# Statistics of four row tiles moved to ScalarE, exponentials in groups of eight, and another order of all pieces

## The chip, the cores and the metric

The kernel runs on one NeuronCore of a Trainium2 chip. Five engines run side by side, each with a queue of its own: TensorE (PE in the profile, with its weight loads as PEld), VectorE (DVE), ScalarE (ACT), GpSimd (POOL) and SyncE (SP, which here only issues DMAs). The metric is the device time of one execution in microseconds.

## The reference, cut to what matters

```python
mod = (_silu(c) @ w_mod).reshape(1, 6, 1, -1)           # sa, ca, ga, sb, cb, gb
h = _layernorm(x) * (1 + ca) + sa                        # x is 2048 x 512
# S4: K[d, l] = Re sum_n C[d,n] exp(dt[d] A[d,n] l) dt[d] B[d,n],   N = 128
# y = irfft(rfft(h, 4096) * rfft(K, 4096))[:2048] + h * Dskip
x = x + ga * y
h = _layernorm(x) * (1 + cb) + sb
r = max(h @ w1 + b1, 0)                                  # w1 512 x 1792
x = x + gb * ((r * r) @ w2 + b2)                         # w2 1792 x 512
```

`_layernorm` takes mean and variance over the 512 columns of a row; dt is exp(log_dt). All data is float32.

## The kernel before, in words

**Stages.** The program is one list of instructions, written piece by piece, and then put in another order by a planner.

1. *Start.* dt is worked out on VectorE from the load `log_dt` (L541 to L551, ending in `dtc`), spread by PE (L554) and copied by ScalarE (L557). From it come, for the first four of eight blocks of channels (HEAD = 4), the parameters (L577 to L624: on ScalarE an arctangent, L604, and sines, L613 and L615; on VectorE a reciprocal, L601; on POOL products and sums), and tables of exponentials (L866, 24 on ScalarE for each group of blocks). Beside it the load `cin` gives silu(c) (L670 to L684) and the modulation (L679 onward), from which come `g1` and `shift` (L704 on ScalarE, L705 on VectorE).
2. *Rows.* x is held as 16 row tiles of 128x512. For each, VectorE takes mean and variance (L661 BN_STATS, L662 BN_AGGR), and four rows at a time POOL adds eps and takes the power -1/2 (L665, L666). Then for each row VectorE subtracts the mean and multiplies by `g1` (L716), ScalarE scales an identity by the row's rstd (L718, "selection", four buffers), PE multiplies (L720, which waits for `shift` once, and 16 of L723) and ScalarE copies the result out of one of three PSUM banks (L726) into `xj`, a part of the buffer `big`.
3. *Kernel and transforms* (61 to some 280 us). K is made in 32 pieces: POOL adds phases (L847, L875) and multiplies amplitudes (L897, L901), ScalarE takes sine and cosine (L885 to L887), VectorE multiplies (L911 to L914), and PE sums over n (L921). PE's transforms go between them: stage one (L772, copied out by ScalarE at L774), stage two (L782), products on VectorE (L932), and back (L940, copied by VectorE at L946).
4. *Second half.* The inverse (L1129), the second layernorm (L1150 onward), and the feed-forward part in two pairs of 4 row groups: first product L1242, with high and low parts of each operand, bias and squares (L1251 to L1254, and L1287), second product L1263 to L1265, and at each end `block_end` (L1272, L1275 add the input rows).

**What sets the order.** `keep_order` takes the groups of instructions and hands them to the engines in a simulated time: of those that are ready, the one that can begin first, with a cost from `weight` and an urgency from the dictionary `urgent`. That is filled by `hurry` (a whole part) and `push` (one piece, by a key such as "amp 5" or "r3"), with numbers in the tables HURRY, PUSH and EAGER. ORDER says which piece of the transforms is written behind which piece of K. Consecutive exponentials are one group there, however many. Within an engine the chip keeps the order that comes out; between engines semaphores hold it. Dependencies stay as they are written.

```python
 661            nc.vector.bn_stats(sts[s % 4], rows[s])
 662            nc.vector.bn_aggr(mv1[:, s, :], sts[s % 4])
...
 665            nc.gpsimd.tensor_scalar(var, var, EPS, None, op0=ALU.add)
 666            nc.gpsimd.tensor_tensor(var, var, rsq, op=ALU.pow)
```

Of the kernel before, what the change touches and what calls it, by code (L numbers as in the profile page):

```python
# [1477 lines left out]
```

## Time and profile before

| | before |
|---|---|
| median of three runs | 625.21 us (624.66 to 626.1) |
| profiled execution, own time | 623.39 us |
| its span | 621.6 us |
| mean granted TensorE clock | 0.987 |
| busy: PE, POOL | 573.8 us (92%), 458.6 us (74%) |
| busy: DVE, ACT | 442.8 us (71%), 413.3 us (66%) |

The own time is what the device counted for the execution that the profiler watched, and the span is from its first instruction to its last; they differ by 1.8 us. A row of the timeline reads: start in us, duration in us, engine, line, operation, output <- input by the program's names, shapes and types, number of instructions in the row, and, in brackets, how long the engine had stood idle and what released it. A row "x24" holds 24 instructions in succession, and its duration is that of all together. In a window's row stand the stretch, its length, the busy time of each engine with its instructions, the granted clock, the DMA share and the bandwidth.

### The profile page before, as it was taken

The numbers are of one execution on the slowest core, as the hardware profiler recorded it, in microseconds if no ns is written. First come the engines' busy times: TensorE is split into PE (matmuls) and PEld (weight loads), VectorE is DVE, ScalarE is ACT, GpSimd is POOL, SyncE is SP. The second block draws the span as 40 slices with busy tenths as digits, with TensorE's granted clock in tenths as the row PEclk, the third lists the DMA queues.
The fourth block names the chain that finished last, engine by engine and source line by source line (L and its number), as shares of the span: only waits on it lengthen the run. The fifth ranks groups of instructions, "written<-read, shape, count | busy, mean of one in ns | idle before, by whom it ended". The sixth has DMA issues, their size and how long they took to land.

```text
span 621.6 us, 21600 instructions
## 1 busy us (share of the span) xinstructions
PE 573.8 (92%) x9390; PEld 490.8 (79%) x9390; DVE 442.8 (71%) x714; ACT 413.3 (66%) x781; POOL 458.6 (74%) x380
## 2 busy tenths in 40 slices
PE   1479998999999999999899999999998999999996
PEld 1346987999999988998677877788886887778875
DVE  6697588899598979855799845458949645456743
ACT  3868999988978777541878656455966545555341
POOL 5649999999998998350754898935798587794351
PEclk9779999999999999999999999999999999999999
DMA  9941003330311063065441432015444253210432
GB/s 317 398 153 38 36 5 72 71 71 4 72 37 38 13 164 90 20 156 174 139 137 34 119 102 69 17 35 159 146 121 134 84 137 102 55 30 34 135 103 84
DMA packets 45838, 60.70 MB, mean 98 GB/s; under 512 B 5168, under 2 KB 26544, under 8 KB 45616
## 3 DMA queue, kind: packets, MB, share of 16 engines
q1 hardware_dynamic: 45312, 59.20, 32.7%
q8 instruction: 73, 1.20, 0.8%
q10 hardware_dynamic: 432, 0.14, 0.1%
q14 instruction: 21, 0.17, 0.1%
HBM read 46.74 MB, written 4.19 MB: 82 GB/s over the span
## 4 chain that ended last, share of the span: by engine, by line
PE 66%; DVE 16%; ACT 10%; POOL 3%; issue 2%; DMA 2%; SPq 0%; DVEq 0%; ACTq 0%
PE ps L940 8%; PE ac L1242 8%; PE ps L782 6%; PE ps L772 6%; PE ps L1242 4%; PE kg L921 3%; PE ac L1264 3%; PE ac L1263 3%; PE ac L1265 3%; PE ps L1263 3%; PE ps L1265 3%; PE ps L1264 3%; PE ps L723 3%; PE kg L1242 2%; ACT tg L885 2%
## 5 line engine op out<-in xcount | busy, mean ns | idle before, releaser
L1211 POOL TENSOR_TENSOR w2r<-xy,w2r 128x512 fp32r<-128x512 f32 x56 | 80.5, 1438 | 64.3 <-ACT w2r L1210 60.8
L782 PE MATMUL ps<-xy,t_sb 128*64 128x64 f32 x1920 | 63.1, 223 | 1.1 <-DVE xy__761 L932 1.0
L782 PEld LDWEIGHTS ps<-xy,t_sb 128*64 128x64 f32 x1920 | 59.9, 138 | 3.1 <-DVE xy__761 L932 1.3
L940 PE MATMUL ps<-e_sb,xy 128*64 128x128 f32 (+2 forms) x768 | 54.6, 261 | 0.3 <-DVE xy L932 0.3
L1210 ACT CAST w2r<-xy 128x512 fp32r<-128x512 f32 x56 | 34.8, 621 | 27.9 <-DMA xy<-w 13.2
L1264 PE MATMUL ac<-w2r,r 128*128 128x512 f32 x112 | 43.7, 390 | 0.1
L1263 PE MATMUL ac<-w2r,r 128*128 128x512 f32 x112 | 43.6, 390 | 0.0
L1265 PE MATMUL ac<-w2r,r 128*128 128x512 f32 x112 | 43.6, 389 | 0.0
L901 POOL TENSOR_TENSOR rtl<-tables 128x1024 f32<-128x1024 f32 x22 | 43.1, 1957 | 0.0
L1242 PE MATMUL ac<-tt,k1t 128*128 128x512 f32 x168 | 41.8, 393 | 0.6
L940 PEld LDWEIGHTS ps<-e_sb,xy 128*64 128x64 f32 x768 | 40.7, 139 | 1.0 <-DVE xy L932 0.5
L940 PE MATMUL ps<-e_sb,xy__761 128*64 128x128 f32 x384 | 38.1, 277 | 1.9 <-ACT xy L774 1.4
L774 ACT COPY xy<-ps 128x512 f32<-128x512 f32 x60 | 34.2, 595 | 6.8 <-PE ps L772 6.8
L1234 POOL TENSOR_TENSOR k1t<-xy,k1t 128x1024 fp32r<-128x1024 f32 x14 | 34.3, 2450 | 6.0 <-ACT k1t L1232 6.0
L1242 PEld LDWEIGHTS ac<-tt,k1t 128*128 128x128 f32 x168 | 31.1, 188 | 9.0 <-DVE xy L1363 2.7
L875 POOL TENSOR_TENSOR rtl<-lo,big 128x1024 int32<-128x1024 int32 x16 | 34.2, 2139 | 4.9 <-DVE big L946 2.8
L1143 POOL TENSOR_TENSOR big<-big,xy 128x512 f32<-128x512 f32 x12 | 16.6, 1403 | 24.5 <-ACT big L1140 24.3
L946 DVE COPY big<-ps 128x256 f32<-128x256 f32 (+1 forms) x66 | 24.4, 408 | 14.5 <-PE ps L940 14.2
L875 POOL TENSOR_TENSOR llph<-lo,big 128x1024 int32<-128x1024 int32 x16 | 34.5, 2158 | 0.0
L1263 PE MATMUL ps<-w2r,r 128*128 128x512 f32 x84 | 33.6, 400 | 0.0
L772 PE MATMUL ps<-d_sb,ksb 128*64 128x128 f32 x512 | 32.9, 275 | 0.4 <-DVE ksb L1005 0.3
L1265 PE MATMUL ps<-w2r,r 128*128 128x512 f32 x84 | 32.8, 391 | 0.0
(300 smaller groups left out, 1751.5 us busy)
## 6 DMA issues: line engine op xcount, KB each, us to landing
xy<-w SPq DMA_DIRECT2D x91, 256.0 KB, 2.8
xy<-xt SPq DMA_DIRECT2D x32, 256.0 KB, 4.1
xy<-xy SPq DMA_DIRECT2D x32, 256.0 KB, 3.5
xy<-w_mod SPq DMA_DIRECT2D x5, 1024.0 KB, 9.3
out_dram<-p SPq DMA_DIRECT2D x16, 256.0 KB, 2.2
t_sb<-c_t SPq DMA_DIRECT2D x1, 2048.0 KB, 11.6
i2c<-c_i SPq DMA_DIRECT2D x4, 512.0 KB, 4.6
big<-prm SPq DMA_DIRECT2D x2, 768.0 KB, 6.0
```

The source lines that it names most:

```text
L772: nc.tensor.matmul(ps[64 * r : 64 * r + 64, 128 * i : 128 * i + 128], src[:, i], d1_sb[:, r], start=True, stop=True)
L782: nc.tensor.matmul(ps[64 * r : 64 * r + 64, 64 * i : 64 * i + 64].rearrange("p (h q t) -> p q h t", h=2, t=2), t2_sb[:, 8 * g + i, r], src ...
L875: nc.gpsimd.tensor_tensor(ph.rearrange("p d r (a b) -> p (d r) a b", a=4), bc(low_phase[:, us].rearrange("p d r b -> p (d r) b"), 2, 4), b ...
L901: nc.gpsimd.tensor_mul(am[:, 0, :, 32:96].rearrange("p d (v x) -> p d v x", v=2), bc(et[:, 256 + 8 * d0 : 384 + 8 * d0].rearrange("p (y a) ...
L940: nc.tensor.matmul(ps[64 * m : 64 * m + 64], pairs(y)[:, g, i // 2, 64 * m : 64 * m + 64, i % 2], e1_sb[:, h].rearrange("p (r j) -> p r j" ...
L1210: nc.scalar.copy(to[:, 0], wst)
L1211: nc.gpsimd.tensor_sub(to[:, 1], wst, to[:, 0].bitcast(F32))
L1234: v.tensor_sub(to[:, 1, 0:4], sum4, f32(to[:, 0, 0:4]))
L1242: nc.tensor.matmul(ps[:, cols], x, y, start=(i == 0 and not onto), stop=(i == 5), skip_group_check=onto)
L1263: pe.append(nc.tensor.matmul(banks[m], r2l[:, ms], hi_, start=(f == 0), stop=False))
L1264: pe.append(nc.tensor.matmul(banks[m], r2h[:, ms], lo_, start=False, stop=False))
L1265: pe.append(nc.tensor.matmul(banks[m], r2h[:, ms], hi_, start=False, stop=(f == NF - 1)))
```

## The change

1. *Statistics.* For rows 12 to 15 (`ON_ACT = (3,)`, the last four) BN_STATS and BN_AGGR are left out. Two passes of ScalarE with a running sum (`accum_out`) take their place: Identity with scale -1/512 sums to the negated mean, and Square with that as bias sums the squared deviations. What the passes write is scrap, into the part of `xj` that the row's copy fills later. The row product then adds the negated mean, and POOL's first instruction multiplies by 1/512 besides adding eps.
2. *Exponentials.* A group of them is at most eight (`EXP_PART = 8`), so the planner can put other instructions between.
3. *Costs.* Changed in the planner: arctangent counts as being in sine's table; costs of small VectorE and POOL instructions and of float32r matmuls; which instructions share the port of VectorE and POOL; a latency on one engine between a write and its use (`LATE`); a first landing time of 800 ns for loads.
4. *Order.* EAGER, HURRY and PUSH hold other numbers, ORDER is written a little differently, and many pieces get keys of their own: "first", "stats", "rstd", "scale", "shift", "row", "second" in the start, "statistics", "prepare", "apart", "w1", "w2", "squares", "end", "ready" in the second half.

```diff
-EAGER = (-9562, 11339, -94586, 321)
+EAGER = (-66075, -100296, -97238, 981)
 ON_DVE = {}
+ON_ACT = (3,)
 PACED = 2
-HURRY = (-1461, -4821, 8205, 112224, 84830, 415716, 138080, -1155)
+EXP_PART = 8
+HURRY = (-5655, 3681, -27793, 1547244, 582933, 1907014, 158015, -98043)
...
-    "00": -56717, "10": -14679, "30": -7223, "40": -6492, "50": -30466, "60": -22657, "A0": 6594, "A1": 1436,
+    "00": -27019, "10": -1752, "20": 1281, "30": -19704, "40": 6869, "50": 735, "A1": -49404, "A2": 83060,
...
-    return {"Exp": 1, "Sin": 2, "Arctan": 3, "Sqrt": 4}.get(str(getattr(ins, "func", "")).split(".")[-1])
+    return {"Exp": 1, "Sin": 2, "Arctan": 2, "Sqrt": 4}.get(str(getattr(ins, "func", "")).split(".")[-1])
...
-        if of and of[-1][0] == eng and (of[-1][1] is None or (kind and of[-1] == key)):
+        if of and of[-1][0] == eng and (of[-1][1] is None or (kind and of[-1] == key and not (kind == "exp" and len(groups[-1]) >= EXP_PART))):
...
-        nc.vector.bn_stats(sts[s % 4], rows[s])
-        nc.vector.bn_aggr(mv1[:, s, :], sts[s % 4])
+        if s // 4 in ON_ACT:
+            none = xj[:, :, 4 * s : 4 * s + 4].rearrange("p d g -> p g d")
+            row = rows[s].rearrange("p (g d) -> p g d", g=4)
+            nc.scalar.activation(none, row, AF.Identity, scale=-1.0 / D, accum_out=mv1[:, s, 0:1])
+            nc.scalar.activation(none, row, AF.Square, bias=mv1[:, s, 0:1], accum_out=mv1[:, s, 1:2])
+        else:
+            nc.vector.bn_stats(sts[s % 4], rows[s])
+            nc.vector.bn_aggr(mv1[:, s, :], sts[s % 4])
...
-            nc.gpsimd.tensor_scalar(var, var, EPS, None, op0=ALU.add)
+            unit = 1.0 / D if s // 4 in ON_ACT else 1.0
+            nc.gpsimd.tensor_scalar(var, var, unit, EPS, op0=ALU.mult, op1=ALU.add)
...
-            nc.vector.scalar_tensor_tensor(row, row, mv1[:, s, 0:1], g1, op0=ALU.subtract, op1=ALU.mult)
+            away = ALU.add if s // 4 in ON_ACT else ALU.subtract
+            nc.vector.scalar_tensor_tensor(row, row, mv1[:, s, 0:1], g1, op0=away, op1=ALU.mult)
```

Line numbers change with it: the first row matmul is L784 for L720, the row copy L790 for L726, the exponentials L933 for L866, the first sine L658 for L613, stage one L839 for L772, the phase L942 for L875, the kernel product L988 for L921.

**What moves.** The counts on PE, POOL and SP are equal; VectorE has 8 instructions less, ScalarE 8 passes and one table load more (10 loads for 9). Three places show the order.

VectorE in the start, at the chain of dt (`kf`, `fr`, `pl`, `ki`, `dtc`), before:

```order
L546 TENSOR_SCALAR pl<-fr 128x4
L548 SCALAR_TENSOR_TENSOR pl<-pl,fr 128x4 x5
L549 TENSOR_SCALAR ki<-kf 128x4
L548 SCALAR_TENSOR_TENSOR pl<-pl,fr 128x4
L551 SCALAR_TENSOR_TENSOR dtc<-pl,ki 128x4
L661 BN_STATS st_75<-xy_94 128x6
L662 BN_AGGR mv_74<-st_75 128x2
```

and now:

```order
L714 BN_STATS st_76<-xy_94 128x6
L593 SCALAR_TENSOR_TENSOR pl<-pl,fr 128x4
L715 BN_AGGR mv_74<-st_76 128x2
L593 SCALAR_TENSOR_TENSOR pl<-pl,fr 128x4
L714 BN_STATS st_77<-xy_94 128x6
L593 SCALAR_TENSOR_TENSOR pl<-pl,fr 128x4
L714 BN_STATS st_78<-xy_94 128x6
L593 SCALAR_TENSOR_TENSOR pl<-pl,fr 128x4
L715 BN_AGGR mv_74<-st_77 128x2
L715 BN_AGGR mv_74<-st_78 128x2
L596 SCALAR_TENSOR_TENSOR dtc<-pl,ki 128x4
```

The statistics of the first four rows stand between the steps of the chain instead of behind it. On ScalarE's DMA queue `cin` is now issued ahead of `ldt`.

ScalarE behind the cast of `shift` (`big_87` holds `xj`, `ps_160` to `ps_162` are the three banks, `tables` the exponentials), before:

```order
L704 CAST shift<-s_317 128x512
L718 ACTIVATE big_86<-ident,mv_74 128x2x64
L726 COPY big_87<-ps_161 128x128x4
L613 ACT_TABLE_LOAD
L613 ACTIVATE big_86<-big_86 128x4x64
L726 COPY big_87<-ps_162 128x128x4
L726 COPY big_87<-ps_160 128x128x4
L718 ACTIVATE big_86<-ident,mv_74 128x2x64 x3
```

and now:

```order
L764 CAST shift<-s_317 128x512
L711 ACTIVATE big_87,mv_74<-xy_97 128x4x128 x2
L712 ACTIVATE big_87,mv_74<-xy_97,mv_74 128x4x128
L711 ACTIVATE big_87,mv_74<-xy_97 128x4x128
L712 ACTIVATE big_87,mv_74<-xy_97,mv_74 128x4x128 x2
L790 COPY big_87<-ps_161 128x128x4
L782 ACTIVATE big_86<-ident,mv_74 128x2x64
L711 ACTIVATE big_87,mv_74<-xy_97 128x4x128
L933 ACTIVATE tables_336<-big_86 128x64 x8
L782 ACTIVATE big_86<-ident,mv_74 128x2x64
L790 COPY big_87<-ps_162 128x128x4
```

The eight passes (L711, L712) and 16 exponentials stand where the sine was, which now follows 30 rows behind the cast, after two table loads; 16 exponentials and the arctangent's chain, which stood ahead of the cast, now stand behind it.

VectorE at the switch between row groups in the feed-forward part (`p` output rows, `ac` banks, `r` squares), before:

```order
L1275 TENSOR_TENSOR p_4619<-p_4619,big_86 128x512 x2
L1287 SCALAR_TENSOR_TENSOR ac_4764<-ac_4764,b1c,p_4619 128x512
L1186 TENSOR_TENSOR tt<-rawh,tt 128x1024
L1253 TENSOR_TENSOR ac_4764<-ac_4764,xy_95 128x512
L1254 TENSOR_TENSOR r_4615<-ac_4764,r_4615 128x512
```

and now:

```order
L1360 TENSOR_TENSOR p_4619<-p_4619,big_86 128x512
L1372 SCALAR_TENSOR_TENSOR ac_4764<-ac_4764,b1c,p_4619 128x512
L1360 TENSOR_TENSOR p_4619<-p_4619,big_86 128x512
L1337 TENSOR_TENSOR ac_4764<-ac_4764,xy_99 128x512
L1372 SCALAR_TENSOR_TENSOR ac_4762<-ac_4762,b1c,p_4619 128x512
L1338 TENSOR_TENSOR r_4615<-ac_4764,r_4615 128x512
```

The product and difference (now L1337, L1338) no longer stand behind L1186 (now L1267), and the bias step L1287 (now L1372) stands between the two additions.

More of the change, by code (lines that the diff above doesn't have):

```diff
@@ L40 @@
 HEAD = 4
-EAGER = (-9562, 11339, -94586, 321)
+EAGER = (-66075, -100296, -97238, 981)
 ON_DVE = {}
+ON_ACT = (3,)
 PACED = 2
-HURRY = (-1461, -4821, 8205, 112224, 84830, 415716, 138080, -1155)
+EXP_PART = 8
+HURRY = (-5655, 3681, -27793, 1547244, 582933, 1907014, 158015, -98043)
 EXPS = [(0, 1), (1, 1), (2, 2), (4, 2), (6, 2)]
 PUSH = {
[41 rows of a table removed]
[75 rows of a table added]
 }
 ORDER = (
-    "rrrrrrrxrrrxrrrrrrpCABBCCBCBCAACB.BBCBAAAAlAC...0aaaa.1.aDaaa..DbbbbEEDD..DEbxbD.b2DDb.EccccccE."
-    ".FEE3ccF..dddd.EdddFF4d.FGG..FeeGeeFG..GexFGHHe5Ge.w.efffGHf.Hf..fH.wwH6fHfgg.g.gHwg..gg7hhhgh"
+    "rrrrrrrxrrrxrrrrrrpCBABCCBCBCAACB.BBCBAAAAlAC.0..aaaa1..aDaaa..DbbbbEDED..DEbxbD.b2DDb.EccccccE."
+    ".FEE3ccF..dddd.EdddF4Fd.FGG..FeeGeeFG..GeFGHHxe5Ge..efffGHf.Hfw..wfH.wH6fHfggw.g.Hgg..ggg7hhhh"
 ).split(".")
@@ L143, in shares_port @@
     of, to = wide(ins.ins), wide(ins.outs)
-    return type(ins).__name__ != "InstBNStats" and all(of) and any(to) | (len(of) > 1)
+    return type(ins).__name__ not in ("InstBNStats", "InstReciprocal") and all(of) and any(to) | (len(of) > 1)
 def function_table(ins):
-    return {"Exp": 1, "Sin": 2, "Arctan": 3, "Sqrt": 4}.get(str(getattr(ins, "func", "")).split(".")[-1])
+    return {"Exp": 1, "Sin": 2, "Arctan": 2, "Sqrt": 4}.get(str(getattr(ins, "func", "")).split(".")[-1])
 def within(ins):
@@ L166, in weight @@
             if ins.ins[0].bass_ap.dtype == FR:
-                t = max(moving / 2.4 + 13, 119)
+                t = max(moving / 2.4 + 15, 121)
                 t += 340 if any(st == 0 for st, _ in ins.ins[0].ap[1:]) else 0
@@ L185, in weight @@
             if n <= 4:
-                t = 120
+                t = 75
             elif type(ins).__name__ == "InstReciprocal":
                 t = 70 + 6.15 * n
+            elif "TensorScalar" in type(ins).__name__ and shares_port(ins) and sum(free_size(a) > 4 for a in operands(ins.ins)) == 1:
+                t = 65 + 0.55 * n + 60 * sum(free_size(a) == 1 for a in operands(ins.ins)[1:])
             elif type(ins).__name__ != "InstBNStats":
@@ L193, in weight @@
             wide = operands(ins.ins)
-            whole = bool(wide) and all(a.ap[-1][0] == 1 and len(a.ap) == 2 for a in wide)
-            t = 140 + (2.13 if whole else 1.91 if str(wide[0].bass_ap.dtype) == str(I32) else 1.75) * n if wide else 70 + 1.2 * n
+            spread = any(st == 0 and k > 1 for a in wide for st, k in a.ap[1:])
+            t = 140 + (2.16 if not spread else 1.92 if str(wide[0].bass_ap.dtype) == str(I32) else 1.75) * n if wide else 70 + 1.2 * n
+            if n <= 4:
+                t = 1020 if len(wide) > 1 else 230
         case _:
@@ L207 @@
 PACKET, FIRST_END = 127.67, 92.2
+LATE = {"PE": 0, "Activation": 90, "DVE": 120, "Pool": 110, "SP": 0}
 def keep_order(tc, traced, slots, in_turn, whole, urgent, behind, follows):
@@ L252, in keep_order @@
     seen, held, left_by = {}, {}, {}
-    before = [set() for _ in groups]
+    before, tight = [set() for _ in groups], set()
     for g, il in enumerate(groups):
@@ L273, in keep_order @@
                             before[g].add(h)
+                            if w and of[h][0] == of[g][0]:
+                                tight.add((h, g))
                             if write and rows | r == rows and cells | c == cells:
@@ L308, in keep_order @@
             ready[of[g][0]].append(g)
-    landed = table = shape = 0
+    landed, table, shape, pool_port = 800, 0, 0, 0
     port = False
@@ L357, in keep_order @@
             port = shares_port(groups[g][0])
-            cost += max(0, free["Pool"] - now) if port else 0
+            cost += max(0, pool_port - now) if port else 0
         elif e == "Pool":
-            cost += max(0, free["DVE"] - now) if port else 0
+            wide = bool(groups[g][0].outs) and hasattr(groups[g][0].outs[0], "bass_ap") and free_size(groups[g][0].outs[0]) > 4
+            cost += max(0, free["DVE"] - now) if port and wide else 0
+            pool_port = now + cost if wide else pool_port
         elif e == "Activation":
@@ L374, in keep_order @@
         for h in after[g]:
-            at[h] = max(at[h], free[e] if of[h][0] == e and not dma else done + (100 if of[h][0] == "PE" else 0))
+            at[h] = max(at[h], free[e] + (LATE[e] if (g, h) in tight else 0) if of[h][0] == e and not dma else done + (100 if of[h][0] == "PE" else 0))
             left[h] -= 1
@@ L654, in tile_adaln_ssm_ffn @@
     spare = [bank("tg", 2)[:, 0:256] for _ in range(2)]
+    fine = mark
     for _ in parameters(0, HEAD, spare):
-        pass
+        push(fine, "first ")
+        fine = len(nc.cur_bb.bb.instructions)
     hurry(mark, HURRY[0])
-    mark = len(nc.cur_bb.bb.instructions)
+    mark = fine = len(nc.cur_bb.bb.instructions)
     for s in range(16):
-        nc.vector.bn_stats(sts[s % 4], rows[s])
-        nc.vector.bn_aggr(mv1[:, s, :], sts[s % 4])
+        if s // 4 in ON_ACT:
[6 more added lines that the diff above has]
+            nc.vector.bn_aggr(mv1[:, s, :], sts[s % 4])
+        push(fine, "stats ")
+        fine = len(nc.cur_bb.bb.instructions)
         if s % 4 == 3:
             var = mv1[:, s - 3 : s + 1, 1]
-            nc.gpsimd.tensor_scalar(var, var, EPS, None, op0=ALU.add)
+            unit = 1.0 / D if s // 4 in ON_ACT else 1.0
+            nc.gpsimd.tensor_scalar(var, var, unit, EPS, op0=ALU.mult, op1=ALU.add)
             nc.gpsimd.tensor_tensor(var, var, rsq, op=ALU.pow)
+            push(fine, "rstd ")
+            fine = len(nc.cur_bb.bb.instructions)
     hurry(mark, HURRY[1])
@@ L703, in tile_adaln_ssm_ffn @@
             g1[:, 128 * q : 128 * q + 128], ident[:, 32 * q : 32 * q + 1].to_broadcast([P, P]), g4, start=True, stop=True)
+    push(mark, "scale ")
+    fine = len(nc.cur_bb.bb.instructions)
     nc.scalar.copy(shift, bc(s4, 1, 4))
     nc.vector.scalar_tensor_tensor(shift, shift.bitcast(F32), second, bc(s4, 1, 4), op0=ALU.mult, op1=ALU.subtract)
+    push(fine, "shift ")
     hurry(mark, HURRY[3])
@@ L715, in row_pieces @@
             mark = len(nc.cur_bb.bb.instructions)
-            nc.vector.scalar_tensor_tensor(row, row, mv1[:, s, 0:1], g1, op0=ALU.subtract, op1=ALU.mult)
+            away = ALU.add if s // 4 in ON_ACT else ALU.subtract
+            nc.vector.scalar_tensor_tensor(row, row, mv1[:, s, 0:1], g1, op0=away, op1=ALU.mult)
+            push(mark, "row ")
+            fine = len(nc.cur_bb.bb.instructions)
             sel = sels[s % 4]
@@ L726, in row_pieces @@
             moved.append(nc.scalar.copy(xj[:, :, 4 * s : 4 * s + 4], ps.rearrange("p (g d) -> p d g", g=4)))
+            push(fine, "r")
             hurry(mark, HURRY[4])
@@ L737, in parameter_pieces @@
         decay(HEAD, NC - HEAD)
+        fine = mark
         for _ in parameters(HEAD, NC - HEAD, (g1[:, 0:256], g1[:, 256:512])):
-            pass
+            push(fine, "second ")
+            fine = len(nc.cur_bb.bb.instructions)
         more.append(1)
@@ L1046, in tile_adaln_ssm_ffn @@
             next(work[t])
-            push(mark, t)
+            if t not in "pr":
+                push(mark, t)
     w2v = w2.rearrange("(t p) d -> p t d", p=P)
@@ L1145, in inverse, with pushed, wrap, g @@
                     paced_load(xts[s + 4], xt[s + 4])
+    def pushed(key):
+        def wrap(f):
+            def g(*a, **k):
+                mark = len(nc.cur_bb.bb.instructions)
+                r = f(*a, **k)
+                push(mark, key)
+                return r
+            return g
+        return wrap
+    @pushed("statistics ")
     def statistics(s):
@@ L1152, in statistics @@
         nc.vector.reciprocal(rstd2[:, s : s + 1], rstd2[:, s : s + 1])
+    @pushed("prepare ")
     def prepare(s, banks, plain_):
@@ L1182, in tile_adaln_ssm_ffn @@
     b11, b12, b21, b22 = rawh[:, 0, 0:2], rawh[:, 1, 0:2], rawh[:, 0, 2:4], rawh[:, 1, 2:4]
+    @pushed("apart ")
     def apart(to, of):
@@ L1202, in tile_adaln_ssm_ffn @@
     w2_made = {}
+    @pushed("w2 ")
     def w2_tile(n):
@@ L1218, in tile_adaln_ssm_ffn @@
     w1s = {}
+    @pushed("w1 ")
     def w1_sums(g):
@@ L1247, in tile_adaln_ssm_ffn @@
     r2 = {}
+    @pushed("squares ")
     def squares(n, ps, rr, b=None):
@@ L1268, in ffn2 @@
             w2_tile(n + 3)
+    @pushed("end ")
     def block_end(k, banks, xos):
@@ L1384, in tile_adaln_ssm_ffn @@
         block_end(2 * pair, acc_b, [p1[:, i] for i in range(4)])
+        @pushed("ready ")
         def ready(n):
```

114 rows, old and new, of the table PUSH are left out of this document.

## The prediction

> **What bounds the kernel now.** I read the shares first, then the windows by stage, then the timeline where TensorE stands still.
>
> ```profile
> span 621.6 us, 21600 instructions
> PE 573.8 (92%) x9390; PEld 490.8 (79%) x9390; DVE 442.8 (71%) x714; ACT 413.3 (66%) x781; POOL 458.6 (74%) x380
> ...
> core 0: us, PE busy (x) PEld busy (x) DVE busy (x) ACT busy (x) POOL busy (x), PEclk, DMA share, GB/s
> 16.00:31.00 15.00, 6.18 (x84) 4.61 (x76) 10.62 (x22) 13.43 (x53) 9.89 (x14) 0.77 1.06 400
> 47.00:62.00 15.00, 14.29 (x325) 10.27 (x323) 10.75 (x19) 12.17 (x29) 14.12 (x14) 1.00 0.13 35
> 280.00:326.00 46.00, 41.02 (x1355) 33.97 (x1352) 36.02 (x88) 26.42 (x72) 21.49 (x17) 1.00 0.51 150
> ...
> 193.98 2.14 POOL L875 TENSOR_TENSOR rtl<-lo,big 128x1024 int32<-128x1024 int32 x1 [1.74 <-ACT tg L887]
> ```
>
> TensorE is busy for 573.8 of 621.6 us, and the change leaves its matmuls as they are, so only the 47.8 us in which it stands still can be won. Over half of that lies ahead of 47 us, where ScalarE (13.43 of 15 us in the second row) carries the work. In the row stage (third row) PE, ACT and POOL are all nearly full, and POOL stays so until about 250 us: the 1.74 us ahead of the phase at 193.98 is its one real gap. About 5 us more are lost between 280 and 326 us (46.00 less 41.02), and 2.88 us at one place near 477 us, shown below.
>
> **The change part by part: the start.**
>
> ```profile
> 4.76 0.17 DVE L541 TENSOR_SCALAR kf<-ldt 128x4 f32<-128x4 f32 x1 [3.06 <-DMA ldt<-log_dt]
> 6.81 0.20 ACT L670 ACTIVATE sl<-cin 128x4 f32<-128x4 f32 x1 [3.27 <-DMA cin<-cvec]
> 7.14 0.16 DVE L551 SCALAR_TENSOR_TENSOR dtc<-pl,ki 128x4 f32<-128x4 f32 x1
> 7.95 0.18 DVE L662 BATCH_NORM_AGGREGATE mv<-st 128x2 f32<-128x6 f32 x1
> 10.20 0.72 POOL L563 TENSOR_TENSOR big<-big 128x256 f32<-128x256 f32 x1 [6.85 <-ACT big L557]
> 10.96 3.67 ACT L866 ACTIVATE tables<-big 128x64 f32<-128x64 f32 x24 [0.84 <-POOL big L563]
> 11.95 2.44 DVE L661 BATCH_NORM_STATS2 st<-xy 128x6 f32<-128x512 f32 x4
> 14.26 1.05 POOL L666 TENSOR_TENSOR mv<-mv,small 128x4 f32<-128x4 f32 x1
> 15.35 1.28 ACT L718 ACTIVATE big<-ident,mv 128x128 f32<-128x128 f32 x4 [0.72 <-POOL mv L666]
> 16.54 0.46 ACT L587 ACTIVATE tg<-big,magic 128x256 f32<-128x256 f32 x1
> 27.58 5.61 ACT L866 ACTIVATE tables<-big 128x128 f32<-128x128 f32 x24
> 32.98 0.63 ACT L704 CAST shift<-s 128x512 fp32r<-128x512 f32 x1
> 34.50 0.74 DVE L705 SCALAR_TENSOR_TENSOR shift<-shift,small,s 128x512 fp32r<-128x512 f32 x1
> 35.29 0.79 PE L720 MATMUL ps<-shift,pick 128*128 128x512 f32 x1 [7.20 <-DVE shift L705]
> ```
>
> Two small loads swap places on ScalarE's DMA queue, so log_dt lands when cin did (6.81 for 4.76: +2.05), and four statistics with their aggregates are woven into the chain that makes dtc (2.44, and four times 0.18: +3.16). The chain ends at 7.30 + 5.2 = 12.5. ScalarE then builds its four selections, which wait for the power on POOL (1.05): about 13.9 to 15.2, and only then copies dt; with POOL's 0.72 the first exponentials start near 16.8 for 10.96, 5.8 later.
>
> The cast of shift nevertheless comes earlier, because fewer instructions stand ahead of it. They were three groups of 24 exponentials, a table load and the arctangent's chain; now they are 24 exponentials (3.67), 16 of the same form (2.45), 16 of the wide form at 5.61/24 = 0.234 (3.74), and four small ones at the 0.46 of L587 (1.84). That is 11.7, so the cast runs from 28.5 to 29.1. VectorE's combination of shift started 0.9 after the cast; I let it follow by 0.4, since the reciprocal moves behind it. The first row matmul starts at about 30.3 for 35.29: **-5.0** at this point.
>
> **The row stage.** Rows 12 to 15 lose four statistics and four aggregates on VectorE (2.44 + 0.72) and get eight summing passes on ScalarE. VectorE was not the last to finish here, so I count nothing for what it loses; ScalarE is the engine that must now carry the stage.
>
> ```profile
> 24.29 1.28 ACT L604 ACT_TABLE_LOAD   x1
> 25.58 0.37 ACT L604 ACTIVATE tg<-tg 128x256 f32<-128x256 f32 x1
> 40.27 0.42 ACT L613 ACTIVATE big<-big 128x256 f32<-128x256 int32 x1
> 43.63 0.73 POOL L616 TENSOR_TENSOR big<-big 128x256 f32<-128x256 f32 x1
> 51.25 1.05 ACT L726 COPY big<-ps 128x512 f32<-128x512 f32 x2
> 57.10 2.13 POOL L875 TENSOR_TENSOR rtl<-lo,big 128x1024 int32<-128x1024 int32 x1
> 58.93 1.08 PE L723 MATMUL ps<-xy,big 128*32 128x128 f32 x32
> 60.72 5.53 PE L772 MATMUL ps<-d_sb,big 128*64 128x128 f32 x94 [0.71 <-ACT big L726]
> ...
> 304.46 0.81 ACT L1159 ACTIVATE xy<-big,mv,rstd 128x512 f32<-128x512 f32 x1
> 318.05 0.63 ACT L1252 ACTIVATE r<-xy 128x512 fp32r<-128x512 f32 x1
> ```
>
> No row shows a pass with a running sum. The nearest passes over 128x512 take 0.525 (two copies in 1.05), 0.63 alone (L1252) and 0.81 with a per-row scale and bias (L1159). I take 0.57, since these passes stand in a run and read SBUF; the ends are 0.525 and 0.81. From the cast to the last row copy ScalarE then has: 8 passes 4.56; 16 copies at 0.525, 8.40; 12 selections at 0.32, 3.84; the last 16 exponentials, 8 x 0.153 + 8 x 0.234 = 3.09; two table loads at 1.28, 2.56 (one more load than before in the program, since arctangent and sine are now in two turns); 13 small ones at 0.37, 4.81. That is 27.3. To it I add the 2.8 that ScalarE stood still in the window from 47 to 62 (15.00 less 12.17). 29.1 + 27.3 + 2.8 = 59.2, against 60.72 for the first matmul of the next stage: **-1.5**. So of the 5.0 won at the start, 3.5 are given back, because the rows are no longer paced by PE (16 rows from 35.29 to 60.01, 1.54 each) but by ScalarE. Bounds: -5.0, if ScalarE's work hides between the rows as before, and +3.3: passes at 0.81 (+1.9) and waits twice as long (+2.8) make +3.2.
>
> The Trainium skill ("ScalarE: Activation LUTs", What ACT_TABLE_LOAD costs) puts a switch at 1283 ns for the load and about 1380 ns for a drain. By that, an estimate, the two switches of this stage would cost 2.8 more, and the sum below would be +0.9 instead of -1.9. The trace agrees on the load and shows no drain behind it: the load at 24.29 took 1.28, and the next activation began at 25.58.
>
> **What is late next: sine and POOL.** The order puts all eight passes, 16 exponentials, eight copies, eight selections, six small ones and both loads ahead of the first sine: 4.56 + 3.09 + 4.20 + 2.56 + 2.2 + 2.56 = 19.2, with 1 for waits 49.2 against 40.27. POOL's product with it moves from 43.63 to some 49.5 (+5.8). The power of rows 12 to 15 (1.05, with its small addition some 1.3), which stood between that product and the first phase, now stands ahead, so the first phase moves from 57.10 to about 61.6, +4.5.
>
> ```profile
> 67.34 1.22 DVE L914 TENSOR_TENSOR rtl<-rtl,tg 128x1024 f32<-128x1024 f32 x1
> 69.18 1.03 PE L921 MATMUL kg<-rtl 128*32 128x64 f32 x58
> ...
> 251.59 1.96 POOL L901 TENSOR_TENSOR rtl<-tables 128x1024 f32<-128x1024 f32 x1
> ...
> 264.04 1.12 PE L921 MATMUL kg<-rtl 128*32 128x64 f32 x64
> ```
>
> The first kernel product at 69.18 had 0.6 to spare (L914 ended at 68.56). The last had more: POOL was done at 253.55, and PE came to it at 264.04. The new order puts two more groups of L772 and two of L782 ahead of the first kernel product, about 3.9 us of PE work. PE then reaches it at 69.18 - 1.5 + 3.9 = 71.6; its data would come at 68.56 + 4.5 = 73.1. That is a wait of 1.5, less what POOL's new order gives back, since it puts several amplitude pieces one or two instructions of 1.96 earlier. I take half: **+0.8**. Bounds: 0, and the whole lateness less POOL's gap, 5.8 - 1.7 = +4.1.
>
> **Behind 264 us.** Between 280 and 326 copies on VectorE are put ahead of aggregates and an inverse matmul group ahead of others. It has 5.0 of idle time to work on, spread over many places. I take **-0.3**, with -1.5 and +1.5 for ends.
>
> ```profile
> 469.84 4.06 DVE L1275 TENSOR_TENSOR p<-p,big 128x512 f32<-128x512 f32 x2
> 473.83 0.75 DVE L1287 SCALAR_TENSOR_TENSOR ac<-ac,b1c,p 128x512 f32<-128x512 f32 x1
> 474.49 1.65 DVE L1186 TENSOR_TENSOR tt<-rawh,tt 128x1024 fp32r<-128x1024 f32 x1
> ...
> 477.59 0.74 PE L1242 MATMUL ac<-h1h,k1t 128*128 128x512 f32 x2 [2.88 <-DVE r L1254]
> ```
>
> At the switch of the row pairs PE waits 2.88 for L1254, behind two slow L1275 and L1186. The new order lets L1254 pass L1186 (1.65), but puts a second L1287 (0.75) ahead of it: **-0.9**. Ends: 0, if L1275 itself is what counts, and -2.9.
>
> **The sum.** -1.5 + 0.8 - 0.3 - 0.9 = -1.9. The profiled execution's own time is 623.39 (span 621.6), so it becomes 621.5; it lies 1.82 below the median of 625.21, which becomes 623.3. 0.2%, or 1.25 us, is about what can be told from no change.
>
> **The rivals.**
> - *POOL late (slower).* The sine's delay of 5.8 reaches the kernel products in full, since POOL has no slack but the 1.7 at 193.98 to catch up. It decides if the first phase starts later than about 63: then each early product waits, and cover like the 0.6 is gone. Price +4.1, less 1.2 from the back: 628.1. For it: POOL's 14.12 of 15 us. Against: the 3.9 of PE work moved ahead, and the cover of some 10 us at the end.
> - *The stage gives nothing.* Passes near 0.81 and more waits on the three banks make ScalarE end at the old 60.7, and L1275 still blocks the pair switch: about 625.2. For it: ScalarE's 27.3 in 30 us leave no room.
> - *All of the early start is kept.* PE stays the pace of the rows: -5.0, less 1.2, with K on time: 619.0. Against it: the same 27.3.
> - *A switch holds ScalarE for longer than its load*, by as much again (1.28) at each of the two: -1.9 + 2.6, about 625.9. The activation that begins at 25.58, right behind the load, speaks against it. (The Trainium skill's drain, named above, is this mechanism.)
>
> **How the numbers follow.** The forecast has 0.46, with a range of its own of 620.5 to 625.0; POOL late 0.24; nothing 0.16; all kept 0.10; the dearer switch 0.04. The range of 618.0 to 629.0 takes in the centres of all five, and leaves out the tails of the first and the third, where several bounds would have to meet. Faster by over 0.2% (below 623.96): 0.35 of the forecast, 0.10 and some 0.05 of the others. Slower (above 626.46): 0.21 of POOL late and 0.06 of the others. The remainder, 0.23, is no change.
>
> **What would show it.** The dtc chain ends near 12.5, the first row matmul is near 30.3, the passes take 0.53 to 0.63, and ScalarE has almost no idle time from 29 to 59. The first L772 (now L839) is near 59.2, the first sine near 49, the first phase near 61.6, and the waits for L914's successor stay below 2 us in all. The pair switch keeps a wait of about 2. The prediction is wrong if K is late over the whole middle of the program (POOL full, PE waiting for VectorE's products), or if the row matmuls still run at some 1.5 a row from 30 us on.

## The result, and the profile after

| | before | changed |
|---|---|---|
| median | 625.65 us (624.66 to 626.24, 4 runs) | 634.21 us (631.81 to 634.55, 4 runs) |
| ratio, with its 95% interval | | 1.0138 (1.0094 to 1.0183) |
| profiled execution: own time, span | 623.39, 621.6 us | 634.43, 632.6 us |

The change costs 8.6 us; 623.3 had been forecast, with 629.0 as the upper end. Here and below a ratio leaves out executions more than 1.5% above the fastest of their kernel, which a median counts. Where the profiled executions differ most is the stretch from the first matmul of stage one to the first of the inverse, called the kernel stage from here on (before, then changed; a window's row has the length, then the busy time of PE):

```profile
60.72:284.48 223.76, 217.84 (x6282) 206.44 (x6282) 178.88 (x291) 179.91 (x285) 195.46 (x143) 1.00 0.27 66
59.42:297.07 237.65, 220.94 (x6282) 207.89 (x6282) 187.23 (x298) 183.60 (x290) 199.72 (x145) 0.99 0.26 63
```

It is 13.9 us longer: PE stands still for 16.7 in it (237.65 less 220.94) where it was 5.9, and needs 3.1 more for as many matmuls. Ahead of it 1.3 us are gained, behind it 1.6. The first lines of the page and, from the table of waits, what TensorE waited for behind the row stage:

```profile
span 632.6 us, 21599 instructions
PE 576.7 (91%) x9390; PEld 496.4 (78%) x9390; DVE 436.9 (69%) x706; ACT 421.3 (67%) x798; POOL 454.1 (72%) x380
...
PE ps L839 <- DVE ksb L1072: 5.7, 1, 5.7
PE ac L1325 <- DVE xy L1448: 2.5, 1, 2.5
PE ac L1325 <- DVE r L1338: 1.2, 1, 1.2
```

A wait's row has total, times and longest. One wait of 5.7 in the kernel stage, which the kernel before did not have, is larger than any there. The timeline at that place, and the windows around it (the column behind POOL's is the granted clock):

```profile
93.54 2.13 POOL L942 TENSOR_TENSOR rtl<-lo,big 128x1024 int32<-128x1024 int32 x1
94.36 1.22 DVE L979 TENSOR_TENSOR llph<-llph,tg 128x1024 f32<-128x1024 f32 x1
95.49 5.23 DVE L827 TENSOR_SCALAR cbc<-cbc 128x4 f32<-128x4 f32 x1
95.64 1.05 POOL L964 TENSOR_TENSOR rtl<-tables 128x512 f32<-128x512 f32 x1
96.66 1.94 POOL L968 TENSOR_TENSOR rtl<-tables 128x1024 f32<-128x1024 f32 x1
98.57 2.12 POOL L942 TENSOR_TENSOR llph<-lo,big 128x1024 int32<-128x1024 int32 x1
100.64 0.67 DVE L980 TENSOR_TENSOR llph<-llph,tg 128x512 f32<-128x512 f32 x1
101.44 1.97 PE L839 MATMUL ps<-d_sb,ksb 128*64 128x128 f32 x16 [5.73 <-DVE ksb L1072]
105.14 1.07 POOL L964 TENSOR_TENSOR rtl<-tables 128x512 f32<-128x512 f32 x1 [4.45 <-PE kg L988]
...
95.00:100.00 5.00, 0.71 (x14) 0.47 (x10) 5.00 (x2) 3.23 (x6) 5.00 (x4) 0.78 0.76 161
100.00:105.00 5.00, 3.56 (x82) 3.14 (x82) 4.24 (x6) 1.54 (x2) 0.69 (x1) 0.54 0.00 0
```

```profile
94.52 0.16 DVE L760 TENSOR_SCALAR cbc<-cbc 128x4 f32<-128x4 f32 x1
94.56 1.95 POOL L901 TENSOR_TENSOR rtl<-tables 128x1024 f32<-128x1024 f32 x1
```

The last two rows are the kernel before. A VectorE instruction on four columns (it adds 1 to the modulation `cbc`, which nothing needs before the second half) took 5.23 us for 0.16. It ended at 100.72, just as the third of three more POOL instructions ended (100.69). Behind it stood the products of the next kernel piece, so PE stood still for 5.73, up to 101.44. The granted clock was 0.78 from 95 to 100 and 0.54 from 100 to 105, and POOL in turn waited 4.45 for PE. (The Trainium skill, "TensorE: Matmul & The Clock Gate", part 1, has the array at half its clock after an idle window of some 3.4 us; the windows at 0.78 and 0.54 agree.)

The start came out nearly as worked in this execution:

```profile
27.08 1.08 ACT L711 ACTIVATE big<-xy 128x512 f32<-128x512 f32 x1
27.96 0.20 ACT L711 ACTIVATION_READ_ACCUMULATOR big<-xy 128x1 f32 x1
...
28.55 0.79 PE L784 MATMUL ps<-shift,pick 128*128 128x512 f32 x1 [3.87 <-DVE shift L765]
...
33.13 0.57 ACT L790 COPY big<-ps 128x512 f32<-128x512 f32 x1
...
49.40 0.42 ACT L658 ACTIVATE big<-big 128x256 f32<-128x256 int32 x1
49.90 0.73 POOL L661 TENSOR_TENSOR big<-big 128x256 f32<-128x256 f32 x1 [4.46 <-ACT big L658]
59.42 0.77 PE L839 MATMUL ps<-d_sb,big 128*64 128x128 f32 x10 [0.71 <-ACT big L790]
60.95 2.15 POOL L942 TENSOR_TENSOR rtl<-lo,big 128x1024 int32<-128x1024 int32 x1
73.31 1.12 PE L988 MATMUL kg<-rtl 128*32 128x64 f32 x64
...
29.00:59.40 30.40, 25.05 (x528) 16.88 (x527) 20.67 (x39) 28.18 (x73) 21.16 (x28) 1.00 0.35 111
```

Stage one began at 59.42 (59.2 forecast), the first sine at 49.40 (49.2), the first phase at 60.95 (61.6). The six passes up to the copy at 33.13 took 1.01 each with the reading of their sums.

But stage one moves between executions by more than was gained. With the start of the kernel before, it began at 58.99 to 61.64 in six profiles (before, before_add_early, before_pair_switch, before_second_half, before_second_half_late_split, late_sine_base), 60.5 in the mean; with the changed start at 59.42, 60.77 and 61.39 in three (after, after_add_accum, add_fused), also 60.5 in the mean. A gain at stage one is not shown.

### The profile page after: what moved, and what is told of

Same layout as the page of the kernel before. It is cut to its first block, busy times and chain, and to the rows that moved or that the text cites. A ratio compares the mean times of both kernels' runs of the same rounds, so it can differ in the third digit from the quotient of the medians.

```text
span 632.6 us, 21599 instructions
## 1 busy us (share of the span) xinstructions
PE 576.7 (91%) x9390; PEld 496.4 (78%) x9390; DVE 436.9 (69%) x706; ACT 421.3 (67%) x798; POOL 454.1 (72%) x380
## 4 chain that ended last, share of the span: by engine, by line
PE 48%; ACT 17%; DVE 13%; DMA 7%; issue 7%; POOL 6%; SPq 0%; ACTq 0%; POOLq 0%; DVEq 0%
PE ac L1325 9%; PE ps L1325 6%; PE ps L839 4%; PE ac L1347 4%; PE ac L1349 4%; PE ac L1348 4%; PE ps L849 4%; ACT tables L933 3%; PE kg L1325 3%; PE kg L988 2%; PE ps L1007 2%; DMA xy<-xt 2%; DMA xy<-w 2%; ACT xy L841 2%; POOL w2r L1293 2%
## 5 line engine op out<-in xcount | busy, mean ns | idle before, releaser
L1293 POOL TENSOR_TENSOR w2r<-xy,w2r 128x512 fp32r<-128x512 f32 x56 | 78.5, 1403 | 81.5 <-ACT w2r L1292 81.5
L839 PE MATMUL ps<-d_sb,ksb 128*64 128x128 f32 x512 | 34.4, 280 | 5.9 <-DVE ksb L1072 5.7
L942 POOL TENSOR_TENSOR rtl<-lo,big 128x1024 int32<-128x1024 int32 x16 | 34.3, 2144 | 5.2 <-ACT tg L954 5.0
L839 PE MATMUL ps<-d_sb,big 128*64 128x128 f32 x512 | 32.4, 275 | 3.8 <-ACT xy L841 1.2
L839 PEld LDWEIGHTS ps<-d_sb,ksb 128*64 128x64 f32 x512 | 28.9, 140 | 7.7 <-DVE ksb L1072 6.0
L942 POOL TENSOR_TENSOR llph<-lo,big 128x1024 int32<-128x1024 int32 x16 | 34.3, 2141 | 0.1
L1347 PE MATMUL ps<-w2r,r 128*128 128x512 f32 x84 | 33.5, 399 | 0.0
```

Of the source, the lines that this page charges most:

```text
L839: nc.tensor.matmul(ps[64 * r : 64 * r + 64, 128 * i : 128 * i + 128], src[:, i], d1_sb[:, r], start=True, stop=True)
L942: nc.gpsimd.tensor_tensor(ph.rearrange("p d r (a b) -> p (d r) a b", a=4), bc(low_phase[:, us].rearrange("p d r b -> p (d r) b"), 2, 4), b ...
L1293: nc.gpsimd.tensor_sub(to[:, 1], wst, to[:, 0].bitcast(F32))
L1347: pe.append(nc.tensor.matmul(banks[m], r2l[:, ms], hi_, start=(f == 0), stop=False))
```

## The experiments

In all of them the order of every engine is written out, not planned, so that only the named edit moves; written out so, the unedited orders are those of the two kernels, instruction for instruction. Diffs with instructions in them are edits of such an order. Ratios are to the kernel before, with 95% intervals. Theory 1 was the blocked addition, theory 2 the dear passes and the late sine.

### The addition without the port: add_fused and after_add_accum

```diff
-            nc.vector.tensor_copy(v, tp[:, 0:128].rearrange("p (q a) -> p q a", q=4)[:, :, 0])
-        nc.vector.tensor_scalar_add(cbc, cbc, 1.0)
+            col = tp[:, 0:128].rearrange("p (q a) -> p q a", q=4)[:, :, 0]
+            nc.vector.tensor_copy(v, col) if v is sbc else nc.vector.tensor_scalar_add(v, col, 1.0)
```

> Changed kernel, every instruction in its order, but the 1 is added to cbc while it is copied out of PSUM, so the little addition L827 in SBUF (5.23 us in the changed kernel, 0.16 before) is gone. Theory 1 (the little addition is blocked by three POOL instructions, and the stall with what follows it is nearly the whole loss): about 626.5, 8 less than the changed kernel; PE waits under 1 us where it waited 5.73. Theory 2 (the dear passes make the sine and POOL late, and the stall only stands where the lateness shows): the wait comes back at the next kernel products, 631 or more.

625.13 us, ratio 1.0030 (1.0002 to 1.0057). The wait of 5.73 is gone (1.19 in its place), and 1.08% of the 1.38% with it.

```diff
-        nc.vector.tensor_scalar_add(cbc, cbc, 1.0)
+        nc.vector.tensor_scalar(cbc, cbc, 1.0, 0.0, op0=ALU.add, op1=ALU.add, accum_out=small[:, 6:7])
```

> Changed kernel in its order, with the little addition L827 at its place and from SBUF to SBUF, but in the form that also writes out a running sum (two operations, the second adds 0; the sum goes to a spare column). If it is the form's claim on the port shared with POOL that is blocked, this form takes about 0.2 to 0.4 us and the time is near 626; if any small VectorE instruction at this place is held up, it takes 5 us again and the time stays near 634.

627.53 us, ratio 1.0067 (1.0038 to 1.0096). At the same place, from SBUF to SBUF, this form took (ns) as long as it does when free:

```profile
L827 DVE TENSOR_SCALAR_CACHE_REDUCE cbc<-cbc x1: 147/147/147, 96.8 to 96.8; 128x4 f32<-128x4 f32 x1
L827 DVE DVE_READ_ACCUMULATOR cbc<-cbc x1: 80/80/80, 96.9 to 96.9; 128x1 f32 x1
...
60.77:292.54 231.77, 218.86 (x6283) 206.16 (x6283) 181.67 (x299) 183.28 (x290) 198.01 (x144) 1.00 0.27 65
```

So it is not the place, nor any small instruction there: it is the form. (The last row is this run's kernel stage.) The Trainium skill ("SBUF — State Buffer", Who interferes with whom) says that copies, casts and TENSOR_SCALAR from SBUF to SBUF can claim the port pair shared with POOL, but not TENSOR_SCALAR's form that writes out a sum. These two runs agree with both halves. By the middles of the intervals the block is worth 4.4 us (1.0138 to 1.0067) to 6.8 us (to 1.0030); their widths leave 1 to 10. The traces agree: in after_add_accum PE waits 1.18 at that place (5.73 in the changed kernel) and is busy for 218.86 us of the kernel stage (220.94), together 6.6 less.

### How long a block lasts: after_add_mid and before_add_early

```diff
 L978 SCALAR_TENSOR_TENSOR llph<-llph,tg_169 128x16x32
+L827 TENSOR_SCALAR cbc<-cbc 128x4
 L979 TENSOR_TENSOR llph<-llph,tg_169 128x16x64
-L827 TENSOR_SCALAR cbc<-cbc 128x4
```

> Changed kernel, with one move: the little addition L827 stands one place earlier on VectorE, ahead of L979, so that it begins near 94.3, over 1 us before the end of POOL's phase L942 (95.67), and no longer 0.2 before that end. Theory 1a (the addition gets the port at the next change of POOL's instruction): it takes some 1.3 us and the time falls by 3 to 7, to 627 to 631. Theory 1b (POOL keeps the port through the whole run of its instructions, to 100.7): it takes 6 us and the time stays at 634 or above.

635.06 us, ratio 1.0138 (1.0097 to 1.0178): theory 1b. (The profiled execution took 638.62.)

```diff
 L759 COPY cbc<-ps_161 128x4
+L760 TENSOR_SCALAR cbc<-cbc 128x4
...
-L760 TENSOR_SCALAR cbc<-cbc 128x4
```

> Kernel before, with one move: the little addition to cbc (L760) stands right behind the copy L759, at about 92.8, in the middle of a POOL instruction, and no longer at 94.5. Theory 1: it takes from 0.8 us (to the end of that POOL instruction) to 5 us (through the next ones), and the time grows by 0.5 to 7 us. Theory 2: 0.16 us as before, and no change (625.4).

626.60 us, ratio 1.0025 (0.9993 to 1.0056): no change that can be told. The two additions, first of after_add_mid, then of before_add_early, with POOL's rows:

```profile
95.45 2.14 POOL L942 TENSOR_TENSOR rtl<-lo,big 128x1024 int32<-128x1024 int32 x1
96.28 6.35 DVE L827 TENSOR_SCALAR cbc<-cbc 128x4 f32<-128x4 f32 x1
100.48 2.13 POOL L942 TENSOR_TENSOR llph<-lo,big 128x1024 int32<-128x1024 int32 x1
```

```profile
89.89 2.13 POOL L875 TENSOR_TENSOR rtl<-lo,big 128x1024 int32<-128x1024 int32 x1
91.28 0.76 DVE L760 TENSOR_SCALAR cbc<-cbc 128x4 f32<-128x4 f32 x1
91.97 1.07 POOL L897 TENSOR_TENSOR rtl<-tables 128x512 f32<-128x512 f32 x1
```

In the first POOL kept the port over four of its instructions (to 102.61); in the second VectorE got it at the first change (92.02), though POOL went on at once. In the unedited kernel before it was not held up at all (0.16 at 94.52), while POOL went from one instruction to the next at 94.56. What decides this is not settled by these runs.

### The statistics alone: add_fused_dve_stats and before_act_stats

```diff
-ON_ACT = (3,)
+ON_ACT = ()
```

(The eight VectorE instructions behind those of rows 8 to 11; the addition as in add_fused.)

> As add_fused, and the statistics of rows 12 to 15 are back on VectorE, behind those of rows 8 to 11; no other move. ScalarE loses the eight passes (8.6 us with the reading of their sums). Theory 1: stage one begins about 4 us sooner (55 for 59.4), K by as much, and half of it or so reaches the end: 623, with 621 and 626 for ends. Theory 2: this is the undoing that counts, and the kernel returns to 625 or below only here, 6 us or more below add_fused.

626.31 us, ratio 1.0018 (0.9988 to 1.0048), not to be told from add_fused. Stage one began at 59.2, where theory 1 had 55; in the profiled execution another TENSOR_SCALAR (L666, whose ten instructions take 0.9 in the median) took 5.62 at 111.5. Such blocks come and go between executions of one program: L666 took 2.28 at 64.8 in the profile of add_fused, and 0.40 at that place in the changed kernel's.

```diff
+        on_act(s) if s > 11 else nc.vector.bn_stats(sts[s % 4], rows[s])
+        None if s > 11 else nc.vector.bn_aggr(mv1[:, s, :], sts[s % 4])
```

> Kernel before, with only the statistics of rows 12 to 15 on ScalarE, six passes right behind the cast of shift and two behind the first row copy; all else in its order. Theory 1: 8.6 us of passes against 8.7 us that ScalarE stood still from 31 to 62, so stage one moves by 0 to 4 us and the end by 0 to 3 (625.5 to 628.5). Theory 2: the first sine moves by 8, POOL has no room to make it up, and the end is 5 us or more later (630 and above).

626.48 us, ratio 1.0021 (0.9999 to 1.0044). Moving the statistics costs the kernel before 1.3 us by the middle of that interval, and may cost nothing. So the passes alone do not cost 5 us or more. But the first sine moved only from 40.27 to 43.77, not by the 8 that theory 2 took for granted (49.40 in the changed kernel), so a sine as late as that is not tested here.

### The second half: before_pair_switch, before_second_half, before_second_half_late_split

```diff
-L1275 TENSOR_TENSOR p_4619<-p_4619,big_86 128x512 x2
+L1275 TENSOR_TENSOR p_4619<-p_4619,big_86 128x512
 L1287 SCALAR_TENSOR_TENSOR ac_4764<-ac_4764,b1c,p_4619 128x512
-L1186 TENSOR_TENSOR tt<-rawh,tt 128x1024
+L1275 TENSOR_TENSOR p_4619<-p_4619,big_86 128x512
 L1253 TENSOR_TENSOR ac_4764<-ac_4764,xy_95 128x512
 L1254 TENSOR_TENSOR r_4615<-ac_4764,r_4615 128x512
+L1186 TENSOR_TENSOR tt<-rawh,tt 128x1024
```

> Kernel before, with VectorE's order at the pair switch as in the changed kernel: the bias step L1287 between the two additions L1275, and L1186 behind L1254. If L1186 and the place of the bias step carry the wait of 2.88, PE waits under 1 there and the time falls by 1.5 to 2.5 (0.3 to 0.4%); by the step of the prediction it falls by 0.9; if the block of L1275 by POOL is what counts, by nothing.

623.75 us, ratio 0.9975 (0.9954 to 0.9996): 1.6 us less. In its profile the wait fell from 2.88 to 2.01 only: one of the additions still took 2.34 (at 472.04), and VectorE then waited 1.31 for ScalarE.

```diff
-every instruction from the inverse on: order of the kernel before
+every instruction from the inverse on: order of the changed kernel
```

> Kernel before up to the inverse (its start, statistics, rows and kernel pieces in its own order); the instructions from the inverse on stand among themselves in the order of the changed kernel. If the loss lies in the kernel stage, it is gone here: 625 within 1.5, with the pair switch 1.6 better and the blocked L1476 2.5 worse. If the second half has a part in it, 628 or more.

620.69 us, ratio 0.9954 (0.9931 to 0.9976). The second half of the change is worth 2.9 us (1.5 to 4.3), more of a gain than expected. It still holds a second blocked instruction, here 4.09 at 552.98, with a wait of 2.54 on PE behind it. In the changed kernel:

```profile
570.55 4.05 DVE L1476 TENSOR_TENSOR r<-rs,r 128x512 fp32r<-128x512 f32 x1 [2.42 <-ACT r L1475]
571.52 1.28 POOL L1293 TENSOR_TENSOR w2r<-xy,w2r 128x512 fp32r<-128x512 f32 x1
572.77 1.29 POOL L1442 TENSOR_TENSOR big<-big,lo 128x512 f32<-128x512 f32 x1
...
577.28 1.65 PE L1325 MATMUL ac<-tt,k1t 128*128 128x512 f32 x6 [2.50 <-DVE xy L1448]
```

```diff
-L1476 TENSOR_TENSOR r<-rs,r 128x512
 L1457 SCALAR_TENSOR_TENSOR ac<-ac,b1c,p 128x512
...
 L1338 TENSOR_TENSOR r<-ac,r 128x512
+L1476 TENSOR_TENSOR r<-rs,r 128x512
```

> As before_second_half, with L1476 behind L1338, so that its block by POOL holds up nothing: 2 to 2.5 less than before_second_half, 622.5 to 624.

617.40 us, ratio 0.9898 (0.9866 to 0.9930): 0.56% less, or 3.5 us for the 2 to 2.5 expected, and the fastest version of this study. In its profile that instruction takes at most 1.8, and PE's longest wait behind 400 us is 0.7.

### The start: early_start, early_start_late_split, all_three

```diff
-cin; ldt                                  # ScalarE's DMA queue
+ldt; cin
-BN_STATS, BN_AGGR between the steps of pl  # VectorE
+BN_STATS, BN_AGGR behind dtc
-L782 x4; L602 COPY; L632; L633; L933 x24  # ScalarE
+L602 COPY; L632; L633; L933 x24; L782 x4
-L721; L722; ...; L608                     # POOL
+L608; L623; L624; L625; L626; L721; L722
```

> As add_fused_dve_stats (no block, statistics on VectorE), and the start is put back as before the change: log_dt loaded first, the chain of dt not woven with statistics, ScalarE's copy of dt ahead of the four selections, POOL's parameter products ahead of the powers. dtc then ends near 7.3 for 11.2 and the exponentials begin near 11 for 15.6. If the early stages carry the rest of the loss, stage one begins 3 us sooner than in add_fused_dve_stats and the time falls by 2 to 3 below it; if the new order of the kernel pieces carries it, stage one is sooner and the time is within 1 us of it.

626.76 us, ratio 1.0014 (0.9985 to 1.0042). Stage one began at 57.6 and the first phase at 57.61, near where it was before the change (57.10), but nothing reached the end: PE stood still for 12.6 us in the kernel stage, against 5.9 before. By the expectation this speaks for the order of the kernel pieces.

> As early_start, with one more move: the low part L1476 that took 4.05 us at 570.5 in the changed kernel, blocked by three POOL instructions, stands behind the square's difference L1338 and so behind the work that PE waits for (2.5 us). If that wait is due to the block, it goes and the time is 2 to 2.5 below early_start; otherwise the same.

(The edit of L1476 above, on early_start.) 621.95 us, ratio 0.9959 (0.9933 to 0.9985): 0.55% less, as in the other pair.

```diff
-the start (up to the row stage): order of the kernel before
+the start: order of early_start
```

> As before_second_half_late_split, and the start (up to the row stage, with VectorE's statistics in all rows) in the order of early_start; the kernel stage stays as before the change. Stage one then begins near 57.6 for 60.7. If the order of the kernel pieces in the change is what eats a gain at the start, this order passes it on: 2 to 3 less than before_second_half_late_split, about 620.5. If POOL or the kernel pieces are the bound anyway, no less than it.

(On before_second_half_late_split. By the traces the orders of PE, POOL and VectorE differ from the base up to the pieces near 96 us, not only up to the row stage.) 625.30 us, ratio 1.0015 (0.9988 to 1.0042): 1.2%, or 7.3 us, more than its base. The first expectation is missed; the second (no less than the base) did not name a loss. Windows of the base first, then of all_three; these two executions took the same time (620.45 and 620.54), so the windows show where PE stands still early on, and not the 7.3:

```profile
62.00:80.00 18.00, 17.94 (x469) 17.21 (x466) 9.96 (x13) 17.75 (x30) 17.61 (x15) 1.00 0.12 47
80.00:100.00 20.00, 18.58 (x654) 16.75 (x648) 16.44 (x28) 18.77 (x28) 20.00 (x14) 1.00 0.27 57
```

```profile
62.00:80.00 18.00, 14.78 (x434) 13.60 (x431) 10.15 (x14) 16.53 (x26) 15.86 (x12) 1.00 0.01 3
80.00:100.00 20.00, 16.76 (x548) 14.97 (x543) 16.31 (x26) 16.76 (x25) 20.00 (x15) 1.00 0.23 49
...
46.23 0.42 ACT L613 ACTIVATE big<-big 128x256 f32<-128x256 int32 x1
57.22 6.33 PE L772 MATMUL ps<-d_sb,big 128*64 128x128 f32 x112 [0.70 <-ACT big L726]
71.12 1.12 PE L921 MATMUL kg<-rtl 128*32 128x64 f32 x64
72.33 1.07 POOL L897 TENSOR_TENSOR rtl<-tables 128x512 f32<-128x512 f32 x1 [1.83 <-PE kg L921]
```

The rows are 4 us sooner (57.22 for 61.24 in the base), the sine is later (46.23 for 39.79), and the first kernel product is later too (71.12 for 69.70). But PE did not wait for its data (the row shows no idle time): it came to it later, with more work of stages one and two ahead of it. Up to 80 us PE waited for ScalarE's copies (1.18, 0.65 and 1.17), and POOL was not full (15.86 of 18.00); it waited 1.83 for that product itself.

In these profiles the kernel stage of all_three takes 231.27 us for 223.93 in its base, as much as in early_start (231.16), although behind 96 us it has the order of the kernel before. So what lengthens it lies ahead of 96 us, in the start or in the order of the first kernel pieces: from stage one to the first kernel product it is 13.9 us in early_start, in all_three and in the changed kernel, and 8.5 in the kernel before. No run puts that order back by itself, so the two are not parted.

### A late sine by itself: late_sine_base, late_sine, late_sine_powers_first, sine_4_late

> The same kernel as before_second_half_late_split, as the base of late_sine on the same chip: 0.985 to 0.993 of the kernel before, if its ratio holds.

615.14 us, ratio 0.9857 (0.9820 to 0.9893).

```diff
-L613 ACTIVATE (sine); ...; L614; ...; L615
+...; L589; L613 ACTIVATE (sine); L614; ...; L718; L615
```

> As late_sine_base, with the first sine and its absolute value 8 places later on ScalarE (near 48.5 for 40.3) and its cosine 3 us later, and nothing else moved: the same number of instructions, the rows in their order. If a late sine alone makes POOL and the kernel pieces late, the first phase begins near 62 for 57.3, PE waits 4 to 6 us more in the kernel stage and the time is 4 to 6 above late_sine_base. If the cover of the later pieces takes it up, as the prediction had it, the time is within 1.5 of it.

625.08 us, ratio 1.0027 (1.0004 to 1.0050): 1.7% more, twice the 4 to 6 expected. POOL's power of rows 12 to 15 stood behind the product that waits for the sine, so the rows were late as well (stage one at 67.70 for 60.45), and the prediction's own list of what is queued behind a wait would have told it.

```diff
+L665; L666          # power of rows 12 to 15
 L616 TENSOR_TENSOR  # waits for the sine
-L665; L666
```

> As late_sine, but POOL's power of rows 12 to 15 stands ahead of the product that waits for the sine (as in the changed kernel), so that the rows are not held up. Stage one begins near 60.5 as in late_sine_base, the first phase near 63. If a late kernel chain alone costs what it is late, PE stands still 4 to 6 us more in the kernel stage and the ratio to the kernel before is 0.994 to 1.0 (late_sine_base 0.986 to 0.990); if the cover takes it up, it is below 0.991.

627.44 us, ratio 1.0012 (0.9985 to 1.0040), above both expected ranges, with the first phase at 63.44. But stage one was late again (65.61), so this run does not part the two causes.

```diff
-L613; L726 x2; L718 x3; L726; L718; L726
+L726 x2; L718 x3; L726; L718; L726; L613
```

> As late_sine_powers_first, with the first sine only 5 to 6 us late on ScalarE (behind the seventh row copy), so that the first phase begins near 59.5 (57 in late_sine_base, 61 in the changed kernel). If the kernel chain's lateness passes on in full, the time is 2 to 3 us above late_sine_base (ratio 0.990 to 0.994); with cover, the same as it.

620.87 us, ratio 0.9907 (0.9879 to 0.9935), with the first phase at 58.80 for 56.76 and stage one 1.1 later. That is 0.1% above the one measurement of its base and 0.5% above the other: 0.6 to 3 us. Whether a cover took up part of these delays can't be told from that, and how much each microsecond of a late sine costs while the rows are on time was not measured.

## Why the prediction was wrong, step by step

- **The start (-1.5).** Stage one came 1.3 sooner in the profiled execution (60.72 to 59.42), but that agreement is luck: over all profiles with the one start and the other it did not move. One term was mis-sized: a pass costs 1.01 with the reading of its sum, not 0.57, outside the bounds of 0.525 to 0.81, and eight take 3.5 more. Against that the shift came 1.75 sooner (28.55 for 30.3), most of it because the chain of dt ended at 11.2 for 12.5. Of the 2.8 allowed for waits 2.2 were needed (28.18 of 30.40 busy). before_act_stats and add_fused_dve_stats say that the statistics are worth 1.3 us or nothing.
- **The kernel stage (+0.8, at most +4.1).** This step failed: the stage grew by 13.9, PE's gaps in it from 5.9 to 16.7. Of that 5.73 is the blocked addition, whose whole price is about 4.4 to 6.8 us of the 8.6. The prediction counted only what is late by its inputs. It moved VectorE and POOL instructions on paper without asking which of them claim the same port, although it quoted two L1275 at 4.06 and called them slow. The bounds took in no such event. The one wait that it did count, for the data of the first kernel product, did not come: PE reached it at 73.31 (71.6 forecast) without waiting, after two waits for ScalarE's copies (1.17 and 0.66) in the work ahead of it.
- **POOL late (0.24).** The sine and the first phase were about as late as worked, short of the 63 at which this rival was to decide, and it is not shown that they cost anything: early_start, with the first phase at its old time, gained nothing. What remains without the block is 12.9 us of gaps for 5.9 (after_add_accum, 231.77 less 218.86), nearly all in waits of 1.3 and less. By all_three their cause lies ahead of 96 us, in the start or in the order of the first pieces; which of the moves there it is stays open. (POOL also had a second gap that the prediction missed, 2.77 at 240.27.)
- **Behind 264 (-1.2).** The sign was right, the size too small: 2.9 us by before_second_half, though a block of L1476 eats 0.56% of it. The pair switch alone is -1.6 (-0.9 forecast).
- **The dearer table switch (0.04).** The load at 48.11 took 1.28 and the sine began at 49.40: no drain here either.

In ratios: the second half gives 0.46% back and the block costs 0.7 to 1.1%. To make up the 1.38% measured, the start and the order of the kernel pieces must together cost another 0.7 to 1.1%. all_three has 1.2% for a similar order, but its start is not that of the changed kernel, so this fits and proves nothing. Two sums of the prediction are off by 0.1 (its 49.2 adds up to 49.3, and the upper bound of the start is +3.2); nothing hangs on them.

## What to carry to other kernels

When an order changes, list the VectorE instructions that read and write SBUF without a PSUM operand, and see what POOL runs at that time in the new order: a four-column addition can hold up the engine for 5 us. Take such operands from PSUM while they are there, or put these instructions where nothing that is waited for stands behind them: moving one instruction (L1476) was worth 0.55%, twice. And a stage that is gained early can be worth nothing at the end: in early_start and all_three stage one came sooner, and the time did not fall.

## What was not expected of the hardware

- POOL kept the port over four of its own instructions while VectorE waited (5.23 and 6.35 us), and over three for L1476 (4.05); elsewhere VectorE got it at the first change. The Trainium skill ("SBUF — State Buffer", Who interferes with whom) has the loser blocked for the whole instruction; here it can be a run of them.
- A ScalarE pass over 128x512 with a running sum is two operations in the profile, 1.08 and 0.20 us, at a pitch of 1.01. The copy of a row tile out of PSUM takes 0.57 (33.13). Whether the sum costs the difference or the pass's scattered output was not tested.
- The granted clock was 0.54 from 100 to 105, around the end of a stall of 5.73, and 1.00 from 105 to 110.
